# First unit in one written order, its second layer on whole float32 weights, and the weight splits moved behind it

## The chip, the cores and the metric

The kernel runs on one core of a Trainium2 chip. A time is the device time of one launch in microseconds (us); three launches before the change took 1181.29 to 1183.06 us, with a median of 1182.4. The traces come from one further launch under the profiler. Engines are named as the profile names them: PE (TensorE, matrix products), DVE (VectorE), ACT (ScalarE), POOL (GpSimd) and SP, whose queue issues every DMA.

## What is computed

```python
# x: (8 batches, 8 heads, 512 tokens, 64), state: (8, 8, 32, 64)
a  = softmax(x @ state.T / 8);   xread = a  @ state      # tokens read the state
a2 = softmax(state @ x.T / 8);   sread = a2 @ x          # the state reads the tokens
x  = concat(xread, sread) -> (8, 544, 512)
xn = (x - mean) / sqrt(var + 1e-6) * g_ln
x  = x + relu(xn @ w_ch1) @ w_ch2                        # 512 -> 2048 -> 512
h  = relu(x @ w_in);  c = conv3(h)                       # 512 -> 1024
out = (h * sigmoid(c)) @ w_out                           # 1024 -> 512
```

The weights arrive as float64, everything else as float32.

## The kernel before, in words

The work up to the second residual goes in nine units: one for the 512 tokens of each batch (units 0 to 7) and one for the 256 state rows of all batches together, which comes before unit 7. A unit has sixteen steps m. L1(u, m) (line 636) multiplies the attention weights `AH`/`AL` with the tile `ZH`/`ZL`, in which state and first weights are already multiplied together, into a PSUM bank `ph`; `relu_parts` (line 631) evicts it as a high part `hH` on ACT and a low part `hL` on DVE. L2(u, m) (line 652) multiplies both with slice m of the second weights into the four banks `acc`. `residual` (line 658) then scales `acc` on DVE, adds it to `XT` and stores it. On PE, a full-precision product of this kind is three matrix products of the type float32r: high times high, high times low, low times high (`three`, line 618). L1 takes six such products of 512 columns, L2 twelve. L1(u, m + 1) is issued ahead of L2(u, m), so that the eviction of one lies under the products of the other.

Unit 0 has work that the others lack, for the weights are made usable in it. A slice of 128 rows, 512 KB of float64, is turned into float32 in three stages: ACT takes the two words of each number apart (lines 199 and 200), DVE puts sign, exponent and mantissa in place (lines 205 and 206), POOL adds the last part (line 207). There are 32 slices, 16 of the first and 16 of the second weights. A slice of the second weights is then split into a high and a low float32r part, on ACT (line 239) and POOL (line 240). `z_first(j)`, four times in unit 0, takes four slices of the first weights: PE multiplies them with `gmean` (line 609, float32, 512 columns), DVE scales them and subtracts the product (line 612), PE multiplies them with the state (line 585), and ACT and DVE evict the result as `ZH` and `ZL` (lines 594 and 595). Their scaled form is stored to DRAM (`w1d`), and later units load it from there into a ring of seven buffers `r0` to `r6` (line 574). Beside this, unit 0 holds the layer norm of its own tokens and the attention of unit 1.

Each engine runs its instructions in one fixed order. In the first part of the launch (the attention of batch 0) and from unit 1 on, that is the order of the Python calls. `START` is such an order for the first part: each letter is one call of a generator. Unit 0 lies between the two and was ordered by a scheduler that goes by a model of the durations.

Of the kernel before, what the change touches and what calls it, by code (L numbers as in the profile page):

```python
# [9 lines left out]
F32 = mybir.dt.float32  # L10
# [32 lines left out]
def kernel(  # L43
# [28 lines left out]
    count = [0]  # L72
    hH = new("hH", [2, S], F32R)
    hL = new("hL", [2, S], F32R)
    XT = {}
# [12 lines left out]


    work = {**{c: f"b{c}" for c in "PQRUV"}, "s": "0"}  # L90

# [3 lines left out]
    RING, RAWS = 7, 5  # L95

    WARM = 8
    START = "s0w1ws0a1bab01ca01cabcabc"

# [501 lines left out]
    def z_first(j):  # L601


        for q in range(KC):
            need(1, KC * j + q)
        w = rounded[2 * j : 2 * j + 2]
        vp = bank()
        for q in range(KC):
            T.matmul(vp, gmean[:, q], w[q // 2][:, q % 2], start=q == 0, stop=q == KC - 1)
        for q in range(KC):  # L610
            t = w[q // 2][:, q % 2]
            V.scalar_tensor_tensor(t, t, gcol[:, q : q + 1], vp, op0=ALU.mult, op1=ALU.subtract)
        z_tiles(0, j, w)
        for g in range(2):
            nc.sync.dma_start(w1d[j, g], flat(w[g]))


# [10 lines left out]
    def hidden(m):  # L628
        return hH[:, m % 2], hL[:, m % 2]

    def relu_parts(m, p):
        h, l = (t[:, : p.shape[1]] for t in hidden(m))
        A.activation(h, p, AF.Relu)  # L633
        V.scalar_tensor_tensor(l, p, 0.0, f32(h), op0=ALU.max, op1=ALU.subtract)  # L634

    def L1(u, m):
        c = slice(P * (m % 4), P * (m % 4) + P)
        if u < NB:
            p = ph[m % 2]
            (wh, wl), (ah, al) = Z[u, m // 4], parts[u]  # L640
            for g in range(2):
                three(p, wh[:, g, c], wl[:, g, c], ah[:, g], al[:, g], g == 0, g == 1)
        else:
# [6 lines left out]
        relu_parts(m, p)  # L650
# [25 lines left out]
    w2 = {}  # L676

# [11 lines left out]

    AHEAD = 4  # L690

    def need(a, m):
        i = place_of[a, m]
        conv_a.ensure(min(i + AHEAD, conv_a.total - 1))
        return conv_a.done[i]

    def temp(i):
# [22 lines left out]
    tc_start.enter_context(tc.manual_schedule())  # L720
    V.memset(f32(hL), 0.0)
    G.memset(s_raw, 0.0)
# [43 lines left out]
    def warm(n):  # L766
        for _ in range(n):
            T.matmul(acc[3], hL[:, 1, :P], hL[:, 0], start=True, stop=True)

    warm(WARM)  # L770
    steps = {
        "s": state_start(),
        "0": tokens_start(0, x0T[0], sets[0]),
        "1": tokens_start(1, x0T[1], sets[1]),
    }
# [8 lines left out]
    tc_start.close()  # L784
    load_state(1)
    banks["free"] = pat

    round_1(craw, c0)
    round_2(craw, c0)

    def states_start():
        starts = [work, {"V": spare[5], "R": spare[6], "s": "1"}]
        E2Ts, z2s = [], []
        for g in range(2):
            sc = bank()
            for ql in range(2):
                q = 2 * g + ql
                for h in range(2):
# [3 lines left out]
                    )  # L802
            E2 = new(starts[g]["R"], [S])
            z2s.append(state_weights(sc, E2, starts[g]))
            E2Ts.append(state_weights_t(E2, starts[g]))
        yield
        srs = [state_read(0, g, E2Ts[g]) for g in range(2)]
        srzs = [state_scale(g, srs[g], z2s[g], starts[g]) for g in range(2)]
        yield
        for g in range(2):  # L810
            state_store(0, g, srzs[g])
        yield
        cp = bank()
        T.transpose(cp[:, :24], c0[:, 0], ident[:24, :24])
        A.activation(cw, cp[:, :24], AF.Copy)


# [52 lines left out]

    units = [*range(NB - 1), NB, NB - 1]
    LAST = units[-1]
    for u, follow in zip(units, [*units[1:], None]):
# [10 lines left out]
        made = []  # L884
        if u == 0:
            made += [(2, z_first, 1), (6, z_first, 2), (10, z_first, 3), (13, z_step, 1, 0)]
        elif u < NB:
            made += [(0, z_step, u, 1), (3, z_step, u, 2), (7, z_step, u, 3)]
            if u != LAST:
                made.append((10, z_step, LAST if follow == NB else follow, 0))  # L890

        def gap(m):
            if made and m >= made[0][0] and banks["held"] is None:
                _, make, *which = made.pop(0)
                make(*which)
            elif u == 0:
                with tc.high_priority(offset=100):
                    next(tasks, None)
            else:
                next(tasks, None)  # L900

        if u == 1:
            tc_start.enter_context(tc.manual_schedule())
        if u == 0:
            for g in range(2):
                token_read(0, g)
            for _ in states_start():
                pass
            z_first(0)
            L1(0, 0)  # L910
        for m in range(M1):
            if m < M1 - 1:
                L1(u, m + 1)
            if u == 0 and m == 3:
                for k in range(LATE, M1):
                    load_weight(place_of[2, k])
            if u == 0 and m == M1 - 4:
                pass_pairs(RING)
            if u == LAST:
# [10 lines left out]
            gap(m)  # L930
            if u == 0:
# [13 lines left out]
            if follow == NB and m % 3:  # L945
                gap(m)
        residual(u, n)
        if u != LAST:
# [3 lines left out]
    def place(m, shape, dt=F32):  # L952
        return new(f"w2_{m}", shape, dt)

# [140 lines left out]
```

## Time and profile before

| what | value |
|---|---|
| median of three launches | 1182.4 us |
| the profiled launch: its own time, its span | 1177.8 us, 1176.0 us |
| PE busy | 1125.9 us (96% of the span) |
| DVE busy | 726.6 us (62%) |
| ACT busy | 444.2 us (38%) |
| POOL busy | 207.8 us (18%) |
| mean granted clock of PE | 0.981 of full speed |

The span runs from the first to the last instruction of the trace; the launch's own time is 1.8 us longer. Shares over the whole span hide the stages: the start differs from the rest, and a table by stretches of the span shows it.

### The profile page before, as it was taken

To read this page: it belongs to the slowest core of one execution; us is meant where nothing else is said; L and a number is where in the kernel's file an instruction comes from. 1 tells how busy PE (TensorE), PEld (TensorE's weight loads), DVE (VectorE), ACT (ScalarE), POOL (GpSimd) and SP (SyncE) were. 2 spreads that over 40 slices of the span, in tenths; PEclk is the share of its full clock that TensorE was granted. 3 is DMA by queue.
4 is the path that set the end of the run, shared out by engine and by line. 5 is a ranking of instruction groups with operands and counts; after the bars stand their busy time and mean duration, and the time that the engine had idled before them with its cause. 6 is when DMAs were issued, how large, how long until landed. Compare 5 with 4: busy or idle time off the path is not lost.

```text
span 1176.0 us, 14628 instructions
## 1 busy us (share of the span) xinstructions
PE 1125.9 (96%) x5459; PEld 863.8 (73%) x5459; DVE 726.6 (62%) x1134; ACT 444.2 (38%) x788; POOL 207.8 (18%) x314
## 2 busy tenths in 40 slices
PE   5698899999999999999989999999999999999997
PEld 4365567777777777777767888788788888888885
DVE  4899666566566475565665622577677666666553
ACT  5665333323233233233233222565344434334332
POOL 2565400000000000000000000265433312213110
PEclk8699999999999999999999999999999999999999
DMA  9643533432243333334314124322112102100001
GB/s 298 206 171 108 158 96 105 108 95 90 72 109 85 81 111 76 78 120 108 95 56 107 38 101 155 119 72 90 37 54 72 37 37 80 37 36 36 1 37 45
DMA packets 129283, 106.31 MB, mean 90 GB/s; under 512 B 103332, under 2 KB 107452, under 8 KB 128188
## 3 DMA queue, kind: packets, MB, share of 16 engines
q1 hardware_dynamic: 129212, 105.37, 29.6%
q8 instruction: 43, 0.70, 0.2%
q14 instruction: 28, 0.23, 0.1%
HBM read 83.85 MB, written 21.50 MB: 90 GB/s over the span
## 4 chain that ended last, share of the span: by engine, by line
PE 80%; DVE 12%; ACT 3%; issue 2%; POOL 2%; SPq 0%; DMA 0%; ACTq 0%; DVEq 0%; POOLq 0%
PE acc L619 14%; PE acc L620 14%; PE acc L621 14%; PE ph L619 7%; PE ph L620 7%; PE ph L621 7%; PE pat L585 2%; PE pat L621 2%; PE pat L619 2%; PE pat L620 2%; PE pat L361 2%; PE ph L647 2%; DVE tn L500 1%; ACT bQ L488 1%; DVE ctmp L206 1%
## 5 line engine op out<-in xcount | busy, mean ns | idle before, releaser
L619 PE MATMUL acc<-hH,w 128*128 128x512 f32 (+1 forms) x576 | 221.6, 395 | 2.2 <-ACT hH L633 2.2
L620 PE MATMUL acc<-hL,w 128*128 128x512 f32 (+1 forms) x576 | 220.4, 383 | 1.8 <-DVE hL L634 1.7
L621 PE MATMUL acc<-hH,w 128*128 128x512 f32 (+1 forms) x576 | 220.1, 382 | 0.0
L634 DVE SCALAR_TENSOR_TENSOR hL<-ph,hH 128x512 fp32r<-128x512 f32 (+1 forms) x144 | 94.2, 657 | 183.4 <-ACT hH L633 183.2
L633 ACT ACTIVATE hH<-ph 128x512 fp32r<-128x512 f32 (+1 forms) x144 | 81.6, 569 | 208.9 <-PE ph L621 171.3
L619 PEld LDWEIGHTS acc<-hH,w 128*128 128x128 f32 x576 | 108.1, 188 | 54.5 <-issue 15.9
L1008 DVE SCALAR_TENSOR_TENSOR w<-w,cw,w 128x544 f32<-128x544 f32 x128 | 109.9, 860 | 38.0 <-POOL w L1006 36.2
L620 PEld LDWEIGHTS acc<-hL,w 128*128 128x128 f32 x576 | 109.2, 190 | 24.3 <-DVE hL L634 4.2
L621 PEld LDWEIGHTS acc<-hH,w 128*128 128x128 f32 x576 | 109.0, 189 | 21.7
L207 POOL TENSOR_TENSOR ctmp<-ctmp,AH 128x512 int32<-128x512 int32 x1 | 1.3, 1304 | 610.7 <-DVE ctmp L206 610.7
L619 PE MATMUL ph<-AH,ZH 128*128 128x512 f32 x256 | 104.3, 408 | 0.7 <-ACT ZH L594 0.7
L620 PE MATMUL ph<-AL,ZH 128*128 128x512 f32 x256 | 100.9, 394 | 0.0
L621 PE MATMUL ph<-AH,ZL 128*128 128x512 f32 x256 | 100.1, 395 | 0.0
L989 ACT ACTIVATE w<-w 128x544 f32<-128x544 f32 x64 | 42.1, 657 | 129.4 <-DVE w L1008 129.4
L996 DVE TENSOR_TENSOR w<-w,w 128x512 fp32r<-128x512 f32 x64 | 49.5, 774 | 42.9 <-ACT w L995 42.1
L990 DVE TENSOR_TENSOR w<-w,w 128x544 f32<-128x544 f32 x64 | 48.8, 762 | 39.5 <-ACT w L989 39.5
L619 PEld LDWEIGHTS ph<-AH,ZH 128*128 128x128 f32 x256 | 48.5, 190 | 19.5 <-issue 6.6
L995 ACT ACTIVATE w<-w 128x512 fp32r<-128x512 f32 x64 | 40.4, 631 | 52.4 <-DVE w L990 47.4
L1006 POOL TENSOR_SCALAR w<-w,cw 128x544 f32<-128x544 f32 x64 | 47.7, 746 | 61.8 <-ACT w L1002 58.4
L621 PEld LDWEIGHTS ph<-AH,ZL 128*128 128x128 f32 x256 | 48.2, 189 | 11.8 <-issue 0.8
L620 PEld LDWEIGHTS ph<-AL,ZH 128*128 128x128 f32 x256 | 48.6, 190 | 9.7
L997 POOL COPY w<-w 128x32 f32<-128x32 f32 x64 | 17.5, 273 | 177.5 <-DVE w L990 177.5
(439 smaller groups left out, 2182.0 us busy)
## 6 DMA issues: line engine op xcount, KB each, us to landing
r<-w1d SPq DMA_DIRECT2D x64, 512.0 KB, 4.5
out_dram<-w SPq DMA_DIRECT2D x34, 256.0 KB, 2.2
w<-in_moe_w_ch_dram SPq DMA_DIRECT2D x16, 512.0 KB, 8.0
r<-in_moe_w_ch_dram SPq DMA_DIRECT2D x16, 512.0 KB, 4.9
x2d<-XT SPq DMA_DIRECT2D x8, 1024.0 KB, 4.9
bP<-in_x_dram SPq DMA_DIRECT2D x112, 64.0 KB, 2.5
bP<-in_x_dram SPq DMA_DIRECT2D x28, 256.0 KB, 3.8
w1d<-r SPq DMA_DIRECT2D x8, 512.0 KB, 2.6
```

What stands on the lines that cost most here:

```text
L361: T.matmul(xr[ql], s[:, 2 * g + ql], a, start=i == 0, stop=i == 2)
L619: T.matmul(o, lh, rh, start=first, stop=False)
L620: T.matmul(o, lh, rl, start=False, stop=False)
L621: T.matmul(o, ll, rh, start=False, stop=last)
L633: A.activation(h, p, AF.Relu)
L634: V.scalar_tensor_tensor(l, p, 0.0, f32(h), op0=ALU.max, op1=ALU.subtract)
L989: A.activation(c, c, AF.Sigmoid)
L990: V.tensor_tensor(c, c, h[:, 1 : SEQ + 1], op=ALU.mult)
L995: A.activation(g[:, 0], c[:, :S], AF.Copy)
L996: V.tensor_tensor(g[:, 1], c[:, :S], f32(g[:, 0]), op=ALU.subtract)
L1006: G.tensor_scalar(c, h[:, 0:SEQ], cw[:, f : f + 1], 0.0, op0=ALU.mult, op1=ALU.add)
L1008: V.scalar_tensor_tensor(c, h[:, k : k + SEQ], cw[:, k * FF + f : k * FF + f + 1], c, op0=ALU.mult, op1=ALU.add,)
```

## The change

Unit 0 is no longer left to the scheduler. Its work is cut into generators, one per kind of work, and the string `START` calls them one after the other, a letter for each call: `a` and `b` are the stages of the conversion, `z` the two halves of `z_first`, `P` the products of unit 0, `T` the attention of unit 1, `N` the layer norm, `L` the token reads, `S` the state reads, `d` later loads, `c` splits.

In unit 0, L2 multiplies the whole float32 slice with a float32 `hH`: one product for each of the four banks instead of three, and no `hL`. Two slices share one buffer (`pair2`). The split of the second weights moves behind unit 0: slices 0 to 5 are split at its end (the letter `c`), slices 6 to 15 in unit 1, slice m + 2 after L2(1, m) from m = 4 on. The low part of a split is now subtracted on DVE instead of POOL.

```diff
...
-    hH = new("hH", [2, S], F32R)
-    hL = new("hL", [2, S], F32R)
+
+    hid = {c: new(f"h{c}", [2, S], F32 if c == "H" else F32R) for c in "HL"}
...
-    START = "s0w1ws0a1bab01ca01cabcabc"
+    START = "ss01abaa0b101aa0b1SabaSbzbaLLzPbSaPNSNbaSbPSbaSPdSPSadbPabNaaddbNzbPzPdNbNaabPNPPTPPaabTTTbaTPabPTbbadzzTbPTabTaabPPTaPaTdbPbbTTPTaTddPabzabPzPTPTaabbTPTPPcccPPbPPPTdPcccNTT"
+    SPLITS = 6
...
     def z_first(j):
 
 
-        for q in range(KC):
-            need(1, KC * j + q)
...
+        yield
...
+    def relu_parts(u, m, p):
+        if u == 0:
+            A.activation(hid["H"][:, m % 2], p, AF.Relu)
+            return
+        if (u, m) == (1, 0):
+            hid["H"] = new("hH", [2, S], F32R)
         h, l = (t[:, : p.shape[1]] for t in hidden(m))
         A.activation(h, p, AF.Relu)
         V.scalar_tensor_tensor(l, p, 0.0, f32(h), op0=ALU.max, op1=ALU.subtract)
...
     def L2(u, m, n):
         h, l = (t[:, :n] for t in hidden(m))
         for d in range(KC):
             c = slice(P * d, P * d + P)
-            three(acc[d][:, :n], w2[m][:, 0, c], w2[m][:, 1, c], h, l, m == 0, m == M1 - 1)
+            if u == 0:
+                T.matmul(acc[d], whole2[m][:, c], h, start=m == 0, stop=m == M1 - 1)
+            else:
+                three(acc[d][:, :n], w2[m][:, 0, c], w2[m][:, 1, c], h, l, m == 0, m == M1 - 1)
+
+    def split_w2(m):
+
+        w = w2[m] = new(slot2(m), [2, DM], F32R)
+        A.activation(w[:, 0], whole2[m], AF.Copy)
+        V.tensor_tensor(w[:, 1], whole2[m], f32(w[:, 0]), op=ALU.subtract)
...
+    w2, whole2, pair2 = {}, {}, {}
+
+    def slot2(m):
+        return f"w2_{(m + 7) % M1}" if m < M1 - 1 else "w2_e"
...
         if a == 2:
-            return None
+            if m % 2 == 0:
+                pair2[m // 2] = new(f"w2_{m // 2 - 1}" if m else "w2_e", [2, DM])
+            whole2[m] = pair2[m // 2][:, m % 2]
+            return whole2[m].rearrange("p (k c) -> p k c", c=P)
         if m % 2 == 0:
             rounded.append(new(f"r{RAWS + m // 2 % 2}", [2, S]))
-        if m + RAWS < M1:
-            load_weight(place_of[1, m + RAWS])
...
-    conv_steps = {"a": conv_a.first, "b": conv_a.second, "c": conv_a.third}
-    for c in START:
-        if c == "w":
-            warm(1)
-        elif c in steps:
-            next(steps[c], None)
-        else:
-            conv_steps[c]()
...
+    def firsts():
+        for _ in range(conv_a.total):
+            conv_a.first()
+            yield
+
+    def seconds():
+        for i, (a, m) in enumerate(order):
+            conv_a.second()
+            if a == 1 and m + RAWS < M1:
+                load_weight(place_of[1, m + RAWS])
+            yield
+
+    def firsts_made():
+        for j in range(KC):
+            yield from z_first(j)
+
+    def products_start():
+        L1(0, 0)
+        yield
+        for m in range(M1):
+            if m < M1 - 1:
+                L1(0, m + 1)
+                yield
+            L2(0, m, S)
+            yield
+        yield from residual(0, S)
+        z_step(1, 0)
...
+    def splits_start():
+        for m in range(SPLITS):
+            split_w2(m)
+            yield
...
+        "S": (states_start(), pat),
+        "z": (firsts_made(), pat),
...
+    for c in START:
+        banks["held"], banks["free"], banks["next"] = None, streams[c][1], turn.get(c, 0)
+        next(steps[c], None)
+        turn[c] = banks["next"]
...
+    splits = {(1, m): [m + 2] for m in range(SPLITS - 2, M1 - 2)}
...
-            if u == 0:
-                w2[m] = need(2, m)
             L2(u, m, n)
-            while u == 0 and made and made[0][0] < 12 and made[0][0] == m:
-                gap(m)
+            for k in splits.get((u, m), ()):
...
```

On PE, in the attention of batch 0 before: `L290`, `L300` and `L325` make the state's reads (`bV`, `w2_13`), `L609` multiplies the first weights (`r5`, `r6`) with `gmean`.

```order
L799 MATMUL pat0_83<-w2_10_34_175,sbd0_36_189 64x256
L799 MATMUL pat0_83<-w2_11_35_176,sbd0_36_189 64x256
L290 MATMUL pat1_84<-ident_8_70,w2_14_53_356 128x128 x4
L300 MATMUL pat0_83<-XT1_15_97,bV_52_350 64x128 x8
L300 MATMUL pat1_84<-XT1_15_97,w2_13_56_366 64x128 x8
L325 MATMUL pat0_83<-ident_8_70,bV_58_388 128x128
L325 MATMUL pat1_84<-ident_8_70,w2_13_60_394 128x128
L814 MATMUL pat0_83<-ident_8_70,cbuf_146 128x24
L609 MATMUL pat1_84<-r5_40_245,gmean_11_73 128x512 x2
L609 MATMUL pat1_84<-r6_45_284,gmean_11_73 128x512 x2
L585 MATMUL pat0_83<-r5_40_245,sbd0_36_189 32x512 x4
L585 MATMUL pat1_84<-r6_45_284,sbd0_36_189 32x512 x4
```

The same place in the changed kernel (its lines are numbered three to seven higher: `L612` is the former `L609`, `L366` the token read of line 361):

```order
L799 MATMUL pat1_84<-w2_10_34_175,sbd0_36_189 64x256
L799 MATMUL pat1_84<-w2_11_35_176,sbd0_36_189 64x256
L612 MATMUL pat0_83<-r5_38_217,gmean_11_73 128x512 x2
L612 MATMUL pat0_83<-r6_46_279,gmean_11_73 128x512 x2
L366 MATMUL acc0_77<-AH0_32_173,s_H_6_68 128x512
L366 MATMUL acc1_78<-AH0_32_173,s_H_6_68 128x512
L366 MATMUL acc0_77<-AH0_32_173,s_L_7_69 128x512
L366 MATMUL acc1_78<-AH0_32_173,s_L_7_69 128x512
L366 MATMUL acc0_77<-AL0_33_174,s_H_6_68 128x512
L366 MATMUL acc1_78<-AL0_33_174,s_H_6_68 128x512
```

The product with `gmean` now stands directly behind the scores of the state (`L799`) and ahead of the token reads; transposes and state reads, which stood ahead of it, come later.

On PE, step m = 4 of unit 0, the second layer before; `acc0` to `acc3` are the four banks, `w2_4_87` is the split slice:

```order
L619 MATMUL acc0_77<-hH_1_63,w2_4_87_577 128x512
L619 MATMUL acc1_78<-hH_1_63,w2_4_87_577 128x512
L619 MATMUL acc2_79<-hH_1_63,w2_4_87_577 128x512
L619 MATMUL acc3_80<-hH_1_63,w2_4_87_577 128x512
L620 MATMUL acc0_77<-hL_2_64,w2_4_87_577 128x512
L621 MATMUL acc0_77<-hH_1_63,w2_4_87_577 128x512
L620 MATMUL acc1_78<-hL_2_64,w2_4_87_577 128x512
L621 MATMUL acc1_78<-hH_1_63,w2_4_87_577 128x512
L620 MATMUL acc2_79<-hL_2_64,w2_4_87_577 128x512
L621 MATMUL acc2_79<-hH_1_63,w2_4_87_577 128x512
L620 MATMUL acc3_80<-hL_2_64,w2_4_87_577 128x512
L621 MATMUL acc3_80<-hH_1_63,w2_4_87_577 128x512
```

and changed, with the last three products of the first layer ahead of it; `w2_1_86` holds slices 4 and 5 whole:

```order
L624 MATMUL ph1_82<-AH0_32_173,ZH1_89_576 128x512
L625 MATMUL ph1_82<-AL0_33_174,ZH1_89_576 128x512
L626 MATMUL ph1_82<-AH0_32_173,ZL1_90_577 128x512
L667 MATMUL acc0_77<-hH_1_63,w2_1_86_543 128x512
L667 MATMUL acc1_78<-hH_1_63,w2_1_86_543 128x512
L667 MATMUL acc2_79<-hH_1_63,w2_1_86_543 128x512
L667 MATMUL acc3_80<-hH_1_63,w2_1_86_543 128x512
```

Twelve products have become four.

On DVE, the end of unit 0 before; `L670` scales the banks, `L672` adds, `L634` is `hL`, `L595` is `ZL`:

```order
L634 SCALAR_TENSOR_TENSOR hL_2_64<-ph0_81,hH_1_63 128x512
L670 TENSOR_TENSOR tn_174_1282<-acc0_77,rs0_72_485 128x512
L670 TENSOR_TENSOR tn_174_1282<-acc1_78,rs0_72_485 128x512
L672 TENSOR_TENSOR XT0_31_172<-XT0_31_172,tn_174_1282 128x512 x2
L670 TENSOR_TENSOR tn_174_1282<-acc2_79,rs0_72_485 128x512
L670 TENSOR_TENSOR tn_174_1282<-acc3_80,rs0_72_485 128x512
L672 TENSOR_TENSOR XT0_31_172<-XT0_31_172,tn_174_1282 128x512 x2
L634 SCALAR_TENSOR_TENSOR hL_2_64<-ph1_82,hH_1_63 128x512
L595 TENSOR_TENSOR ZL1_176_1319<-pat1_84,ZH1_175_1318 128x512
L595 TENSOR_TENSOR ZL1_176_1319<-pat0_83,ZH1_175_1318 128x512
```

and changed; `L675` is the new subtraction of a split, `L689` and `L692` the residual, `L600` and `L644` the former `L595` and `L634`:

```order
L675 TENSOR_TENSOR w2_7_155_1017<-w2_e_56_321,w2_7_155_1017 128x512
L675 TENSOR_TENSOR w2_8_156_1020<-w2_e_56_321,w2_8_156_1020 128x512
L675 TENSOR_TENSOR w2_9_157_1023<-w2_0_60_378,w2_9_157_1023 128x512
L210 TENSOR_SCALAR ctmp1_150_962<-ctmp1_150_962 128x512
L211 SCALAR_TENSOR_TENSOR ctmp1_150_962<-w2_15_142_887,ctmp1_150_962 128x512
L689 TENSOR_TENSOR tn_158_1048<-acc0_77,rs0_62_397 128x512
L689 TENSOR_TENSOR tn_158_1048<-acc1_78,rs0_62_397 128x512
L689 TENSOR_TENSOR tn_158_1048<-acc2_79,rs0_62_397 128x512
L689 TENSOR_TENSOR tn_158_1048<-acc3_80,rs0_62_397 128x512
L692 TENSOR_TENSOR XT0_31_172<-XT0_31_172,tn_158_1048 128x512 x4
L600 TENSOR_TENSOR ZL0_167_1105<-pat0_83,ZH0_166_1104 128x512
L600 TENSOR_TENSOR ZL0_167_1105<-pat1_84,ZH0_166_1104 128x512
L675 TENSOR_TENSOR w2_10_170_1114<-w2_0_60_378,w2_10_170_1114 128x512
L675 TENSOR_TENSOR w2_11_171_1117<-w2_1_86_543,w2_11_171_1117 128x512
L675 TENSOR_TENSOR w2_12_172_1120<-w2_1_86_543,w2_12_172_1120 128x512
L644 SCALAR_TENSOR_TENSOR hL_2_64<-ph0_81,hH_173_1129 128x512
```

Three splits stand ahead of the residual and three behind it, ahead of the first `hL` of unit 1.

## Rows read from the trace of the kernel before

**Rows 1.** Busy time by stretch: start:end, length, PE, PEld, DVE, ACT, POOL, PEclk, DMA, GB/s

```profile
20.00:40.00 20.00, 9.44 (x28) 5.71 (x28) 17.74 (x26) 14.51 (x29) 9.93 (x8) 0.59 0.80 236
40.00:60.00 20.00, 13.57 (x67) 7.66 (x67) 16.94 (x32) 12.49 (x24) 6.71 (x6) 0.69 0.73 246
60.00:80.00 20.00, 18.75 (x87) 11.63 (x86) 18.63 (x28) 14.19 (x24) 12.44 (x10) 1.00 0.60 210
80.00:100.00 20.00, 16.15 (x64) 12.02 (x63) 19.78 (x25) 10.93 (x20) 16.08 (x12) 0.91 0.46 131
...
120.00:140.00 20.00, 17.37 (x61) 12.43 (x62) 14.07 (x20) 7.30 (x13) 12.63 (x9) 0.91 0.56 130
```

**Rows 2.** Timeline of PE, 20 to 62: start, duration, instruction, idle before

```profile
24.07 1.11 PE L456 MATMUL pat<-ident,bU 128*128 128x128 f32 x4 [7.47 <-DVE bU L450]
...
47.35 1.11 PE L290 MATMUL pat<-ident,w 128*128 128x128 f32 x4 [4.27 <-ACT w L284]
...
53.96 3.70 PE L609 MATMUL pat<-r,gmean 128*128 128x512 f32 x8
...
61.47 0.50 PE L619 MATMUL ph<-AH,ZH 128*128 128x512 f32 x1
```

**Rows 3.** Timeline of POOL, 30 to 38

```profile
31.94 1.62 POOL L207 TENSOR_TENSOR r<-ctmp,r 128x512 int32<-128x512 int32 x1 [1.02 <-ACT XT L363]
...
35.63 1.40 POOL L207 TENSOR_TENSOR XTt<-XTt,w 128x512 int32<-128x512 int32 x1 [0.63 <-DVE XTt L206]
```

**Rows 4.** Timeline of DVE, 35 to 139

```profile
35.92 1.66 DVE L206 SCALAR_TENSOR_TENSOR ctmp<-w,ctmp 128x512 int32<-128x512 int32 x1
...
54.27 0.69 DVE L206 SCALAR_TENSOR_TENSOR ctmp<-r,ctmp 128x512 int32<-128x512 int32 x1
...
138.26 2.72 DVE L612 SCALAR_TENSOR_TENSOR r<-r,gcol,pat 128x512 f32<-128x512 f32 x4 [3.01 <-PE pat L609]
```

**Rows 5.** Timeline of PE, 92 to 173

```profile
92.19 1.08 PE L273 MATMUL pat<-bQ,sbd 128*64 128x512 f32 x4 [3.85 <-DVE bQ L369]
...
95.33 0.63 PE L621 MATMUL acc<-hH,w 128*128 128x512 f32 x1
...
134.63 3.59 PE L609 MATMUL pat<-r,gmean 128*128 128x512 f32 x8
...
141.04 0.39 PE L621 MATMUL acc<-hH,w 128*128 128x512 f32 x1
141.27 0.39 PE L619 MATMUL acc<-hH,w 128*128 128x512 f32 x1
...
172.91 0.50 PE L619 MATMUL acc<-hH,w 128*128 128x512 f32 x1
```

**Rows 6.** Groups of DVE instructions, 0 to 175: busy, mean ns, idle before

```profile
L205 DVE TENSOR_SCALAR ctmp<-ctmp 128x512 int32<-128x512 int32 x22 | 14.8, 675 | 1.5 <-ACT ctmp L199 1.5
L634 DVE SCALAR_TENSOR_TENSOR hL<-ph,hH 128x512 fp32r<-128x512 f32 x18 | 12.2, 682 | 8.5 <-ACT hH L633 8.5
L206 DVE SCALAR_TENSOR_TENSOR ctmp<-r,ctmp 128x512 int32<-128x512 int32 x11 | 12.2, 1107 | 0.2
```

**Rows 7.** Groups of POOL instructions, 0 to 175

```profile
L240 POOL TENSOR_TENSOR w<-ctmp,w 128x512 fp32r<-128x512 f32 x11 | 15.2, 1392 | 1.5 <-ACT w L239 1.5
...
L240 POOL TENSOR_TENSOR w<-XTt,w 128x512 fp32r<-128x512 f32 x5 | 7.1, 1425 | 0.3 <-ACT w L239 0.3
```

**Rows 8.** Timeline of ACT, 144 to 146

```profile
144.56 1.09 ACT L594 ACTIVATE ZH<-pat 128x512 fp32r<-128x512 f32 x2 [5.00 <-PE pat L585]
```

**Rows 9.** Timeline of SP's DMA issues, 35 to 164

```profile
35.59 4.62 SPq L141 DMA_DIRECT2D s_raw<-in_state_dram  x8
...
159.27 4.05 SPq L158 DMA_DIRECT2D bP<-in_x_dram  x8
```

**Rows 10.** DMA issues of the page: count, KB each, us to landing

```profile
r<-w1d SPq DMA_DIRECT2D x64, 512.0 KB, 4.5
```

**Rows 11.** Line 670: shortest, median and longest ns, first and last start

```profile
L670 DVE TENSOR_TENSOR tn<-acc,rs x28: 680/692/692, 168.6 to 664.3; 128x512 f32<-128x512 f32 x28
```

More of the change, by code (lines that the diff above doesn't have):

```diff
@@ L802, in states_start @@
                     )
[L803 to L809, printed above, removed]
+            E2s.append(new(starts[g]["R"], [S]))
+            z2s.append(state_weights(sc, E2s[g], starts[g]))
+            yield
+        for g in range(2):
+            E2T = state_weights_t(E2s[g], starts[g])
+            yield
+            sr = state_read(0, g, E2T)
+            srzs.append(state_scale(g, sr, z2s[g], starts[g]))
+            yield
         for g in range(2):
             state_store(0, g, srzs[g])
-        yield
+            yield
+        round_1(craw, c0)
+        round_2(craw, c0)
         cp = bank()
@@ L815, in states_start, with reads_start, loads_start, warm_steps @@
         A.activation(cw, cp[:, :24], AF.Copy)
+    def reads_start():
+        for g in range(2):
+            token_read(0, g)
+            yield
+    def firsts():
+        for _ in range(conv_a.total):
+            conv_a.first()
+            yield
+    def seconds():
[3 more added lines that the diff above has]
+                load_weight(place_of[1, m + RAWS])
+            yield
+    def firsts_made():
[3 more added lines that the diff above has]
+        L1(0, 0)
+        yield
+        for m in range(M1):
+            if m < M1 - 1:
+                L1(0, m + 1)
+                yield
+            L2(0, m, S)
+            yield
+        yield from residual(0, S)
+        z_step(1, 0)
+    def loads_start():
+        load_state(1)
+        yield
+        for m in range(LATE, M1):
+            load_weight(place_of[2, m])
+            yield
+        pass_pairs(RING)
+    def splits_start():
+        for m in range(SPLITS):
+            split_w2(m)
+            yield
+    def warm_steps():
+        while True:
+            warm(1)
+            yield
+    streams = {
+        "s": (state_start(), acc),
+        "0": (tokens_start(0, x0T[0], sets[0]), acc),
+        "1": (tokens_start(1, x0T[1], sets[1]), acc),
+        "a": (firsts(), acc),
+        "b": (seconds(), acc),
+        "L": (reads_start(), acc),
+        "S": (states_start(), pat),
+        "z": (firsts_made(), pat),
+        "P": (products_start(), pat),
+        "T": (attend(1), pat),
+        "N": (token_norm(0), pat),
+        "d": (loads_start(), acc),
+        "c": (splits_start(), acc),
+        "w": (warm_steps(), acc),
+    }
+    turn = {}
+    steps = {c: s[0] for c, s in streams.items()}
+    for c in START:
+        banks["held"], banks["free"], banks["next"] = None, streams[c][1], turn.get(c, 0)
+        next(steps[c], None)
+        turn[c] = banks["next"]
+    banks["free"], banks["held"] = pat, None
     x2, x2raw = {}, {}
@@ L884 @@
         made = []
-        if u == 0:
-            made += [(2, z_first, 1), (6, z_first, 2), (10, z_first, 3), (13, z_step, 1, 0)]
-        elif u < NB:
-            made += [(0, z_step, u, 1), (3, z_step, u, 2), (7, z_step, u, 3)]
+        if u < NB:
+            made += [(0, u, 1), (3, u, 2), (7, u, 3)]
             if u != LAST:
-                made.append((10, z_step, LAST if follow == NB else follow, 0))
+                made.append((10, LAST if follow == NB else follow, 0))
         def gap(m):
             if made and m >= made[0][0] and banks["held"] is None:
[L894 to L898, printed above, removed]
+                z_step(*made.pop(0)[1:])
             else:
                 next(tasks, None)
[L902 to L910, printed above, removed]
         for m in range(M1):
@@ L946 @@
                 gap(m)
-        residual(u, n)
+        for _ in residual(u, n):
+            pass
         if u != LAST:
@@ L952, in place @@
     def place(m, shape, dt=F32):
-        return new(f"w2_{m}", shape, dt)
+        return new(slot2(m), shape, dt)
     hb = [place(m, [HB]) for m in range(3)]
```

39 lines of the change are left out of this document (9 added, 30 removed).

## The prediction

> **What bounds the kernel now.** I read the table of busy time by stretches first [rows 1]. PE is busy 9.4 and 13.6 of 20 us up to 60 us, at a granted clock of 0.59 and 0.69, and 16 to 19 in the later stretches shown. DVE is busy 17 to 20 us of each stretch between 20 and 100. So the start is the one stage in which PE, which sets the pace of everything later, waits; whole units behind it are alike, since the six gaps between the residuals of units 0 to 6 add up to 664.3 - 168.6 = 495.7 us, 82.6 each [rows 11]. What a shorter start saves is saved at the end, if nothing in unit 1 eats it.
>
> Then the timeline of PE up to 62 us [rows 2]. It waits 7.5 us for the token softmax, and later 4.3 us in the state's softmax, one of several such waits there. The product with `gmean` starts at 53.96 and the first product of unit 0 at 61.47. Yet the four slices that this `gmean` needs are complete when POOL ends its fourth piece, at 31.94 + 1.62 = 33.56 [rows 3]. They lie ready for 20 us, because the fixed order of PE has the state's reads ahead.
>
> The stretch that I count goes from the first product of unit 0 (61.47) to the first L2 of unit 1 (172.91): 111.4 us [rows 2, 5]. Each 512-column product of the float32r kind takes 0.229 us from start to start (141.04 to 141.27). A float32 product of the `gmean` kind appears as two instructions: eight take 3.59 us, and less the last one's tail that is 0.857 us for a product (their eight starts are 0.43 apart; four products, 3.43 us) [rows 5]. The order has in this stretch 316 products of the first kind (72.4 us), 12 of the second (10.3), 40 small ones of line 585 (5.2), and transposes, scores and state reads (5.3): 93.2 us of work. The other 18.2 us are waits and low clock. An example is the wait of 3.85 us for DVE at 88.3; after it PE's products are 0.43 apart instead of 0.23, that is 1.2 instead of 2.4 GHz, and they last 0.63 us [rows 5].
>
> **The change part by part.** *L2 of unit 0* loses 16 x 12 float32r products, 192 x 0.229 = 44.0 us, and gains 16 x 4 float32 products, 64 x 0.857 = 54.8: 10.8 us more for PE. It is on the path, since PE leads there.
>
> *The new order* takes some work from before the first product of unit 0 to behind it: 16 state-read products, 8 transposes and a few small ones, some 3.4 us by the durations of the same rows. Work from the first product of unit 0 to the first L2 of unit 1 becomes 93.2 + 10.8 + 3.4 = 107.4 us.
>
> *The first product of unit 0* now follows the `gmean` of the first four slices, which stands right behind the scores. The fourth piece is rounded at about 30 us: before it is 33.56, and the softmax's idle on DVE is now filled by two conversions. Then come the last quarter of `gmean` (0.86, or 1.7 at the low clock), the twelve token reads (2.7 or 5.2), which hide DVE's four scalings of 2.72 us [rows 4], line 585 (1.1 or 2.1) and an eviction (0.55 us each, two in 1.09) [rows 8] with about 0.1 of delay. That gives 35.3 us at full clock and a piece at 30; 43.3 at low clock and a piece at 33.56. I take 41, near the late end, since the clock before was 0.59 and 0.69 there [rows 1].
>
> *The DVE* loses 16 evictions `hL` of 682 ns, 10.9 us [rows 6], and gains the splits, 16 subtractions, for which the nearest row is the same 0.68: three ahead of the residual (2.0 us), three behind it, ten in unit 1. *POOL* loses 16 subtractions, 15.2 + 7.1 us [rows 7]. That matters for DVE: line 206 takes 0.69 us while POOL rests, and 1.66 when it starts at 35.92 while POOL's addition runs from 35.63 to 37.03 [rows 3, 4]. So a conversion costs DVE its lines 205 and 206, 0.68 and 1.11 us in the largest groups [rows 6], some 1.73 on the mean of all, and 1.1 if POOL never stands in the way. I keep 1.73, although fewer POOL instructions remain.
> The Trainium skill, "SBUF — State Buffer", section "SBUF: two separate sides", says that DVE and GpSimd share a port pair that one of them holds for a whole instruction while the other is blocked. The trace agrees: the 1.66 ends when POOL's ends, plus 0.55. By that rule the missing 16 POOL instructions free DVE of more than I count, which is the first rival.
>
> *PE's waits in the new order.* (a) Second `gmean`: PE reaches it 16.2 us after the start (four L1, two L2, small ones), at 57.2. DVE has 20 us to do between the first `ZL` (42.5) and the last slice that it needs: six conversions (10.4) and 9.6 of norm, state and `ZL`; with POOL's 1.5 that is 64.0, and the last quarter ends at 64.9 where 60.6 would do: 4 us. (b) Then L2(0, 2) covers part of the scaling, but DVE has five other instructions ahead of it: 2.7. (c) Third `z_first`: nothing stands between `gmean` and line 585 on PE, so 2.72 of scaling, line 585 and the first evictions lie open, less some transposes: 2.9. (d) Third and fourth `gmean` wait 0.5 and 1.3 for POOL; the fourth `z_first` is covered by a product of 3.43 but for its eviction, 0.9. (e) Unit 0 ends with the token read, whose banks ACT has to clear (1.1 [rows 8]), then the state product of unit 1, `ZH`, and `ZL` behind the residual's eight DVE instructions of 0.69 (the first can begin while PE still works on the other banks): 1.9. The splits there run on ACT and DVE beside it. Sum 14.2. (f) Two of the waits throw PE to the low clock, as the one of 3.85 us did; that one ended at 92.19 and the product at 95.33 is still slow [rows 5], so about 3.7 us at half speed, which lose 1.85 each: 3.7. All in all 17.9 us, against 18.2 before.
>
> *Unit 1* gets ten splits, 0.69 on DVE and 0.55 on ACT each. They stand after a step's L2, when ACT and DVE wait for the next L1. Covered, they cost 0; each one whole in the way of an `hL` would cost 6.9. I take 0.6.
>
> Sum: 41 + 107.4 + 17.9 = 166.3 for the first L2 of unit 1, against 172.9: 6.6 us earlier, less 0.6: 6.0. The profiled launch goes from 1177.8 to 1171.8; the launches without the profiler stand 4.6 us above it, so the median goes from 1182.4 to 1176.4.
>
> **The rivals.** *First: DVE gets freer than I count.* Without POOL's 16 subtractions a conversion costs 1.3, between 1.1 and 1.73. The wait (a) loses 2.6, (b) and (d) about 3, and with shorter waits both falls of the clock (3.7): the loss is 8.6 instead of 17.9. With 40 for the start, PE arrives at 156: 16.9 earlier, 1182.4 - 16.3 = 1166. For it speaks the pair of rows with 0.69 and 1.66; against it, that DVE's scalings behind `gmean` remain.
>
> *Second, slower: the low clock.* Every one of the seven waits above throws PE back to 1.2 GHz, and then L2's products cost 1.71 instead of 0.857. Seven falls of 1.85 and 14.2 of waits are 27.2 us. The change loses from 172.9 - 41 - 107.4 = 24.5 us on; so it is 2.7 late, and with 0.6 in unit 1 the median is 1185.7. For it speaks the clock of 0.59 to 0.69 in the start [rows 1]; against it, that between 60 and 80 us it was 1.00 although PE was idle for 1.2 us of them.
> The Trainium skill, "TensorE: Matmul & The Clock Gate", section "HAM oscillation — how this bites in real kernels", tells of kernels in which every repeated wait returns PE to the low clock. The 3.85 us wait agrees with it; by that rule this rival is what happens.
>
> *Third, no change: SP's queue.* The state product of unit 1 needs `r0` and `r1` reloaded. SP issues this behind eight transfers of `bP`, which wait for a state read after L2(0, 11), and sixteen of the state: 4.05 + 2 x 4.62, then 4.5 to land: 17.8 us [rows 9, 10]. PE has three L1 and four L2 until then and a token read, 4.1 + 13.7 + 1.4 = 19.2. The margin is 1.4; if transfers that queue with them take 7.4 longer, margin and gain are gone, and the end is 1182.4.
>
> **How the numbers follow.** The forecast, 1171 to 1180, gets 0.50; the first rival 0.20; the third 0.15; the second 0.15. Differences of 0.2% (2.4 us) are about what can be told from no change here: faster 0.70, same 0.15, slower 0.15. The range goes from 1165, the first rival, to 1185, short of the whole of the second.
>
> **What would show it.** Right: the first `ph` product near 41 us (61.47 before); 128 instructions of the L2 line in unit 0, 0.43 apart; the first residual near 158 (168.6 before); the first L2 of unit 1 near 166; then units of 82.6. Wrong: a first product of unit 0 after 46; PE idle over 4 us in one piece; a granted clock under 0.9 between 60 and 160 (second rival); PE waiting for `r` from `w1d` at the unit's end (third); `hL` in unit 1 late behind a split.

## The result, and the profile after

The changed kernel takes 1164.8 us (median of four launches, 1163.2 to 1165.4); the kernel before 1181.9 (four launches). The ratio is 0.986, with a 95% interval of 0.9833 to 0.9886: 17 us faster, where 6 were forecast. The direction came as forecast; the size did not, and the median stands 0.2 us under the low end of the range. The price that comes nearest is that of the first rival, 1166.

The trace of the changed kernel has a span of 1163.6 us against 1176.0, 12.4 less. First its table by stretches, which answers to [rows 1] (columns as there).

```profile
20.00:40.00 20.00, 16.63 (x76) 9.73 (x76) 16.98 (x32) 13.47 (x26) 6.01 (x5) 0.81 0.92 276
40.00:60.00 20.00, 18.68 (x83) 10.04 (x82) 18.17 (x31) 11.71 (x23) 9.04 (x8) 1.00 0.35 114
60.00:80.00 20.00, 19.73 (x66) 9.21 (x64) 18.53 (x28) 11.53 (x20) 5.71 (x5) 1.00 0.70 232
80.00:100.00 20.00, 18.07 (x75) 7.98 (x74) 15.88 (x25) 8.94 (x16) 6.50 (x5) 1.00 0.52 170
...
120.00:140.00 20.00, 18.83 (x83) 9.44 (x82) 12.68 (x23) 6.68 (x13) 3.95 (x3) 1.00 0.32 82
```

PE is busy 16.6 and 18.7 us where it was 9.4 and 13.6, and from 40 to 160 us its granted clock is 1.00 in every stretch. DVE is as full as before up to 80 us, and less full later.

Then PE's timeline (start, duration, instruction, idle before and what ended it), which answers to [rows 2, 5].

```profile
28.41 3.67 PE L612 MATMUL pat<-r,gmean 128*128 128x512 f32 x8 [0.42 <-ACT bR L289]
...
36.60 0.50 PE L624 MATMUL ph<-AH,ZH 128*128 128x512 f32 x1 [0.64 <-ACT ZH L599]
...
49.39 0.33 PE L330 MATMUL pat<-ident,w 128*128 128x128 f32 x1 [1.32 <-DVE w L320]
...
55.22 3.59 PE L612 MATMUL pat<-r,gmean 128*128 128x512 f32 x8
...
89.78 1.13 PE L612 MATMUL pat<-r,gmean 128*128 128x512 f32 x2 [0.73 <-POOL r L212]
91.75 1.71 PE L590 MATMUL pat<-r,sbd 64*32 64x512 f32 x8 [0.84 <-DVE r L615]
...
103.60 0.33 PE L330 MATMUL pat<-ident,bV 128*128 128x128 f32 x1 [0.61 <-DVE bV L320]
...
124.73 0.50 PE L624 MATMUL ph<-AH,ZH 128*128 128x512 f32 x1 [0.69 <-ACT ZH L599]
...
152.33 1.55 PE L590 MATMUL pat<-r,sbd 64*32 64x512 f32 x16 [0.46 <-ACT XT L368]
...
158.37 0.50 PE L624 MATMUL acc<-hH,w 128*128 128x512 f32 x1
```

The first product of unit 0 starts at 36.60 instead of 61.47, the first L2 of unit 1 (the last row) at 158.37 instead of 172.91: 14.5 us earlier. Between the two PE has ten waits, 5.9 us in all; the longest of them is 1.32. Before, between the same two products, it had six, 8.7 us in all. Next the residuals (shortest, median and longest ns, first and last start; line 670 is now 689), and two groups of the conversion on DVE (line 205 is now 210, 206 is 211):

```profile
L689 DVE TENSOR_TENSOR tn<-acc,rs x28: 690/691/692, 147.9 to 651.7; 128x512 f32<-128x512 f32 x28
```

```profile
L210 DVE TENSOR_SCALAR ctmp<-ctmp 128x512 int32<-128x512 int32 x22 | 11.0, 502 | 0.9 <-ACT ctmp L204 0.9
...
L211 DVE SCALAR_TENSOR_TENSOR ctmp<-r,ctmp 128x512 int32<-128x512 int32 x11 | 8.9, 807 | 0.4
```

The first residual starts at 147.9, where I had it near 158, and the last at 651.7, 12.6 us before the 664.3 of [rows 11]. So 14.5 us are won at unit 1's first L2; unit 1 from there to its residual takes 76.9 us against 75.7 and gives 1.2 back, and the units behind it another 0.8. The mean of line 210 is 502 ns where it was 675, of line 211 807 where it was 1107 [rows 6]: over all groups of the two lines a conversion costs DVE 1.39 us instead of 1.73.

### The profile page after: what moved, and what is told of

Same layout as the page of the kernel before. It is cut to its first block, busy times and chain, and to the rows that moved or that the text cites. A ratio compares the mean times of both kernels' runs of the same rounds, so it can differ in the third digit from the quotient of the medians.

```text
span 1163.6 us, 14521 instructions
## 1 busy us (share of the span) xinstructions
PE 1128.9 (97%) x5393; PEld 845.3 (73%) x5393; DVE 720.9 (62%) x1134; ACT 442.2 (38%) x788; POOL 182.3 (16%) x298
## 5 line engine op out<-in xcount | busy, mean ns | idle before, releaser
L644 DVE SCALAR_TENSOR_TENSOR hL<-ph,hH 128x512 fp32r<-128x512 f32 (+1 forms) x128 | 83.4, 655 | 172.9 <-ACT hH L643 172.5
L624 PE MATMUL acc<-hH,w 128*128 128x512 f32 (+1 forms) x480 | 189.0, 394 | 0.0
L625 PE MATMUL acc<-hL,w 128*128 128x512 f32 (+1 forms) x480 | 181.8, 379 | 0.0
L626 PE MATMUL acc<-hH,w 128*128 128x512 f32 (+1 forms) x480 | 181.8, 379 | 0.0
L643 ACT ACTIVATE hH<-ph 128x512 fp32r<-128x512 f32 (+1 forms) x128 | 72.7, 568 | 196.3 <-PE ph L626 158.9
L624 PEld LDWEIGHTS acc<-hH,w 128*128 128x128 f32 x480 | 90.3, 188 | 44.7 <-issue 15.6
L626 PEld LDWEIGHTS acc<-hH,w 128*128 128x128 f32 x480 | 90.2, 188 | 18.2
L625 PEld LDWEIGHTS acc<-hL,w 128*128 128x128 f32 x480 | 90.3, 188 | 16.7 <-DVE hL L644 0.3
L667 PE MATMUL acc<-hH,w 128*128 128x512 f32 x112 | 50.4, 594 | 0.0
```

The source lines that it names most:

```text
L624: T.matmul(o, lh, rh, start=first, stop=False)
L625: T.matmul(o, lh, rl, start=False, stop=False)
L626: T.matmul(o, ll, rh, start=False, stop=last)
L667: T.matmul(acc[d], whole2[m][:, c], h, start=m == 0, stop=m == M1 - 1)
```

## The experiments

Each was timed in five rounds beside the kernel before on the same chip; medians of the kernel before were 1179.8 to 1181.5 there. The changed kernel's own 1164.8 comes from its first launches; timed once more at the end it took 1166.2, so a difference from it is good to some 1.5 us. The questions: which part brings the 17 us, and by what path.

**Order and arithmetic apart.** The first of two kernels keeps the new order and goes back to the old arithmetic.

```diff
-            if u == 0:
-                T.matmul(acc[d], whole2[m][:, c], h, start=m == 0, stop=m == M1 - 1)
-            else:
+            if True:
                 three(acc[d][:, :n], w2[m][:, 0, c], w2[m][:, 1, c], h, l, m == 0, m == M1 - 1)
...
             conv_a.second()
+            while conv_a.n2 < (i if i < 2 * M1 - 1 else 2 * M1):
+                third()
...
```

The step `third` splits a slice as before, the high part on ACT, the low part on POOL.

> The new order with the old arithmetic in unit 0: L2 as three float32r products a slice, hL made by DVE, each second weight split on ACT and POOL as it is converted. PE has 10.8 us less to do than in the changed kernel, DVE 10.9 us more (16 of 0.68), POOL 22.3 us more. Theory (the whole weights pay by what they take from DVE and POOL, which PE would wait for): PE's idle in unit 0 grows from 5.9 us to 16 or more, a granted clock of 0.5 comes back in places, and the time is 1166 to 1174. Rival (the order is all of the gain, the float32 products only cost): idle stays near 6 us and the time falls by about 10 us, to 1153 to 1157.

Measured: 1206.5 us, ratio 1.022 (1.0201 to 1.0241). Both expectations were too low; the rival is out. The groups of its waits from 30 to 195 us (who waited for what, us in total, times, longest):

```profile
POOL ctmp L212 <- DVE ctmp L211: 36.8, 7, 12.0
DVE hL L639 <- ACT hH L638: 28.5, 12, 4.9
ACT ctmp L204 <- POOL w L245: 20.5, 8, 5.5
ACT hH L638 <- PE ph L626: 17.4, 8, 6.8
...
POOL w L245 <- ACT w L244: 11.5, 4, 5.5
```

The old arithmetic makes a ring of waits: DVE stands for `hH`, which ACT makes from PE's `ph`; ACT stands for a temporary that POOL's subtraction holds; POOL stands for ACT's high part and, longest of all, for DVE's conversions. The places of the splits in this order were my own, so the 42 us over the changed kernel are the price of this order with them, not of every order.

The second keeps the old order (with its scheduler in unit 0) and takes the new arithmetic.

```diff
         if a == 2:
-            return None
+            if m % 2 == 0:
+                pair2[m // 2] = new(f"w2_{m // 2 - 1}" if m else "w2_e", [2, DM])
+            whole2[m] = pair2[m // 2][:, m % 2]
+            return whole2[m].rearrange("p (k c) -> p k c", c=P)
...
+    splits = {(0, 13): (0, 1, 2), **{(1, m): [m + 2] for m in range(4, M1 - 2)}}
```

> The old order with the new arithmetic: L2 of unit 0 with whole float32 weights, no hL, six slices split around unit 0's end, ten in unit 1. The first product of unit 0 stays near 61.5. Theory (the order brings the gain, the arithmetic alone does not): 10.8 us more for PE, of which at most the 8.8 us idle of the kernel before can be won back: 1182 to 1190, not under 1180. Rival (the arithmetic is the gain, since it frees DVE and POOL): 1165 to 1174.

Measured: 1186.0 us, ratio 1.0046 (1.0029 to 1.0063). The arithmetic alone costs 5.5 us, as the theory had it: 10.8 more for PE, half of it won back. The trace agrees: from the first product of unit 0 to the first L2 of unit 1 it takes 116.6 us, 5.2 more than before, with 4.7 us of waits on PE instead of 8.7 and a granted clock of 1.00 in every stretch from 80 us on, where two of [rows 1] have 0.91. So neither half, as built here, is a gain by itself, and together they win 17: the whole weights take away the waits that the early order ran into with the old arithmetic.

**What the removed DVE and POOL work was worth.** Three kernels put it back into the changed one, one kind at a time, with outputs that nothing reads. First the evictions `hL` of unit 0:

```diff
             A.activation(hid["H"][:, m % 2], p, AF.Relu)
+            V.scalar_tensor_tensor(hid["L"][:, m % 2], p, 0.0, hid["H"][:, m % 2], op0=ALU.max, op1=ALU.subtract)
             return
```

> The changed kernel plus the 16 hL evictions of unit 0 on DVE, which nothing reads: 10.9 us more for DVE, nothing for POOL or PE. If PE waits for DVE's sum of work, its idle between the first product and the first L2 of unit 1 grows by 4 us or more, up to 10.9: 1169 to 1176. If DVE has slack: 1164 to 1167.

Measured: 1181.8 us, 17 over the changed kernel; the whole gain is gone, more than the 10.9 us of work that came back. Its group of line 639, up to 180 us (busy, mean ns, idle before), and two of PE's waits:

```profile
L639 DVE SCALAR_TENSOR_TENSOR hL<-ph,hH 128x512 fp32r<-128x512 f32 x16 | 11.0, 685 | 18.5 <-ACT hH L638 18.5
```

```profile
97.13 1.12 PE L612 MATMUL pat<-r,gmean 128*128 128x512 f32 x2 [1.97 <-POOL r L212]
...
132.46 2.07 PE L612 MATMUL pat<-r,gmean 128*128 128x512 f32 x2 [4.20 <-POOL r L212]
```

DVE works 11.0 us on them and stands 18.5 us ahead of them. It runs its queue in order: the conversions behind an `hL` can't begin until PE has made `ph` and ACT `hH`, though they need neither. So DVE can't get ahead of PE, the last slices reach `gmean` late, and PE, which set the pace, waits in its turn. From the first product of unit 0 to the first L2 of unit 1 it takes 138.8 us by the trace, 17.0 more than in the changed kernel. None of PE's listed waits there is for an `hL` itself. The next kernel takes away that wait and leaves the work: the same number of instructions of the same kind and length, in the same places, on a tile at rest.

```diff
             A.activation(hid["H"][:, m % 2], p, AF.Relu)
+            l = f32(hid["L"][:, m % 2])
+            V.scalar_tensor_tensor(hid["L"][:, m % 2], l, 0.0, l, op0=ALU.max, op1=ALU.subtract)
             return
```

> The changed kernel plus 16 instructions on DVE in the places of the hL evictions of unit 0, of the same kind and length (some 0.69 us), but on a tile that is at rest: they wait neither for ACT nor for PE. Theory (what the evictions cost is DVE's wait for hH, in order, 18.5 us in the run that put them back, and not their 11 us of work): 1164 to 1169. Rival (the sum of DVE's work decides): as the run that put the evictions back, 1178 to 1182.

Measured: 1171.7 us (1170.7 to 1174.5).

```profile
L640 DVE SCALAR_TENSOR_TENSOR hL<-hL 128x512 fp32r<-128x512 f32 x16 | 10.9, 679 | 0.0
```

The busy time is the same, 10.9 us, the idle ahead of it 0.0. It lies between the two expectations: some 6.9 us of the 17.0 come with the work, some 10.1 with the wait. The traces give nearly the same shares: from the first product to the first L2 of unit 1 this kernel takes 128.3 us, 6.5 more than the changed one. The work's share holds a wait of PE of 1.96 us for POOL at the third `gmean`, and a granted clock of 0.50 from 94 to 98 us behind it. Then POOL's sixteen subtractions:

```diff
             conv_a.second()
+            if a == 2:
+                kc = lambda v: v.rearrange("p (k c) -> p k c", c=P)
+                G.tensor_tensor(kc(hid["L"][:, m % 2]), conv_a.tmp[i], kc(whole2[m]), op=ALU.subtract)
```

> The changed kernel plus 16 subtractions on POOL, one behind each converted second slice, whose output (in hL's place) nothing reads: some 22 us of POOL work as before, no more for DVE or PE. If DVE is freed by POOL's missing instructions (the first rival of the prediction, lines 210 and 211 stretched from 1.1 to 1.7 us while POOL runs), lines 210 and 211 get longer by 0.4 us and more a slice and PE's idle in unit 0 grows by 4 us or more: 1169 to 1176. If DVE has slack enough for it: 1164 to 1167.

Measured: 1170.5 us (1168.6 to 1171.3), 5.7 over the changed kernel. The time is where the first theory put it, but not by its path: line 211 goes from 807 to 884 ns, and a conversion costs 1.48 us instead of 1.39, not 0.4 more.

```profile
L211 DVE SCALAR_TENSOR_TENSOR ctmp<-r,ctmp 128x512 int32<-128x512 int32 x11 | 9.7, 884 | 0.4
```

So in the new order the missing subtractions explain 0.09 of the 0.34 us by which a conversion became shorter. That does not leave the rest to the order alone: the two kernels that changed one half each both have shorter conversions.

```profile
L206 DVE SCALAR_TENSOR_TENSOR ctmp<-r,ctmp 128x512 int32<-128x512 int32 x11 | 7.9, 725 | 0.1
```

```profile
L211 DVE SCALAR_TENSOR_TENSOR ctmp<-r,ctmp 128x512 int32<-128x512 int32 x11 | 7.6, 693 | 0.4
```

The first row is of the old order without the subtractions, the second of the new order with the old arithmetic and POOL's subtractions; over all groups a conversion takes 1.49 and 1.35 us there. Alone, then, the one takes off 0.24 us and the other 0.38, and both together 0.34: they do not add up. The second of these kernels waits much more, which by itself lets fewer instructions meet; which ones no longer do is not shown. The first L2 of unit 1 comes 6.0 us later (164.37), after 9.1 us of waits instead of 5.9 and one spell at the lower clock (0.57 from 95 to 99 us).

**The early first product.** The two steps of the first `z_first` and two L1 stand behind the state's reads again:

```diff
-... SabaSbzbaLLzPbSaPNSNbaSbPSbaSPdSPS ...
+... SabaSbbaLLbSaNSNbaSSzzPPbPbaSPdSPS ...
```

> The changed kernel with the first product of unit 0 put back: in the emitted order the two steps of the first z_first stand behind the state's reads, and the first two L1 behind them, as in the kernel before; all else as changed. First product near 50 to 54 instead of 36.6. If the early first product is worth what it is early (PE's own work sets the time from there on): 14 to 17 us slower, 1179 to 1182. Rival (DVE's conversions set the pace of unit 0, and they go on meanwhile): 1166 to 1172.

Measured: 1175.3 us (1172.1 to 1177.1), between the two. The first product starts at 50.57, 14.0 later, and the first L2 of unit 1 at 167.14, 8.8 later. Part of the 14 is only moved: state reads that now stand ahead of it stood behind it. The rest is waiting as of old, in front of them:

```profile
35.65 1.97 PE L305 MATMUL pat<-XT,bV 128*64 128x128 f32 x16 [4.95 <-ACT bV L297]
...
40.52 1.97 PE L305 MATMUL pat<-XT,w 128*64 128x128 f32 x16 [1.85 <-ACT w L297]
```

So the earlier first product is worth about two thirds of what it is earlier: 8.8 of 14.0 us by the trace.

**Can more be had?** Four kernels tried, and one joined two of them. Nine products that nothing reads, in PE's waits for the token softmax (`wwwwwww` and `ww` in `START`):

> The changed kernel plus nine products that nothing reads in PE's waits for the token softmax (18 to 23 us), where the granted clock is 0.5 until 27.6. If the low clock delays the first product of unit 0: the state's scores (3.5 us at 24.5) take half, the first product moves from 36.6 to about 35, and the time falls to 1163 or 1163.5. Rival (the fourth rounded piece and the softmax set that start): 1164.5 to 1166.

Measured: 1164.3 us (1163.5 to 1165.5). The granted clock of the stretch from 20 to 40 rises from 0.81 to 0.93, the first product comes at 35.97; 0.5 us is not to be told from nothing. Slices 13 to 15 back on three products:

```diff
-            if u == 0:
+            if u == 0 and m in THREE:
+                three(acc[d][:, :n], w2[m][:, 0, c], w2[m][:, 1, c], h, l, m == 0, m == M1 - 1)
+            elif u == 0:
...
```

> The changed kernel, with slices 13 to 15 split in unit 0 ahead of their L2, which is three float32r products again, with hL on DVE: 36 products of 0.229 us instead of 12 of 0.857, 2.0 us less for PE, and three splits fewer in unit 1. Where DVE idles (5.7 us at 134, 5.0 us at 143) an hL should cost nothing: 1162 to 1163.5. Rival (hL ties DVE and the residual behind it to PE here too): 1165 to 1168.

Measured: 1167.2 us (1165.8 to 1169.0), the time of the rival, but not its path. PE waits twice, and not for an `hL` but for the high part of a split, which it had not needed in unit 0 (line 683 is the split on ACT, 627 the first of the three products):

```profile
141.17 0.51 PE L627 MATMUL acc<-w,w 128*128 128x512 f32 x1 [1.20 <-ACT w L683]
150.52 0.51 PE L627 MATMUL acc<-w,w 128*128 128x512 f32 x1 [1.79 <-ACT w L683]
```

These 3.0 us are more than the 2.0 that the products save; the 1.0 that is left over lies within what can be told, so it is shown only that nothing is gained. The low part of the splits on POOL (`G` for `V` in `split_w2`):

> The changed kernel with the low part of all 16 splits subtracted on POOL instead of DVE (six at unit 0's end, ten in unit 1). Unit 1 from its first L2 to its residual took 76.9 us against 75.7 before. If the ten splits on DVE cost that 1.2: 1163 to 1164. If they are covered: 1164.5 to 1166. If POOL's longer subtraction holds DVE up at the unit's end: 1166 to 1168.

Measured: 1164.5 us (1163.8 to 1165.9), no change that can be told; unit 1 takes 76.3 us instead of 76.9. Three swaps of a scaling step with a conversion:

```diff
-... NSNbaSbPSbaSPd ... PTabTaabPP ... zPTPTaabbTPTPP ...
+... NSNbaSPSbbaSPd ... PTaTbaabPP ... zPTPTaabTbPTPP ...
```

> The changed kernel with three swaps in the emitted order: each time the step that scales a state read stands ahead of a conversion that it stood behind. PE waits for its output for 1.32, 0.61 and 0.48 us (at 49.4, 103.6 and 133.6), and line 318 takes 0.98 us on the mean beside POOL's addition, 0.23 without. If those waits go and nothing else becomes late: 2 us faster, 1162 to 1163.5. Rival (the conversions moved behind become late for the second gmean): 1165 to 1168.

Measured: 1164.3 us (1162.7 to 1165.2). The three waits are gone, but new ones of 1.22 and 0.35 us have come (at 51.3 and 116.7), and from the first product to the first L2 of unit 1 it is 120.8 us against 121.8. Last, these two together, beside the changed kernel itself:

> The changed kernel once more, unchanged, as the measure for the run beside it on the same chip: 1163 to 1166. If its launches, unlike those of the kernel before, have one granted clock, they lie within 3 us of each other.

> The three swaps of the scaling steps and the splits' low part on POOL together. Each alone came out 0.4 and 0.5 us under the changed kernel's median, which is not to be told from nothing. If the waits removed are worth their 1 us at unit 1's first L2 and add up with the splits: 1162 to 1163.5, and under the run beside it. Rival (no gain, launches scatter by as much): within 0.7 us of the run beside it.

Measured: 1166.2 us (1165.8 to 1167.1) for the changed kernel and 1164.5 (1162.7 to 1165.4) for the two edits. Beside each other the launches do not overlap. But the 1.8 us is below the 0.2% that I called the least difference to be told, it was measured once, and the changed kernel's first four launches (1163.2 to 1165.4) lie where those of the two edits lie. A gain is not shown.

## Why the prediction was right in direction and wrong in size

Forecast was 1176.4, measured 1164.8, 11.6 apart. They come from these steps:

- **The first product, 41 forecast, 36.6 measured: 4.4 us.** The steps of the sum were right: the fourth piece is rounded at 29.88 (28.59 + 1.29), "about 30".

```profile
28.59 1.29 POOL L212 TENSOR_TENSOR r<-ctmp,r 128x512 int32<-128x512 int32 x1 [2.03 <-DMA w<-in_moe_w_ch_dram]
```

  What failed is "near the late end, since the clock before was 0.59 and 0.69 there". From 28 us on the granted clock is 1.00, and the eight instructions with `gmean` take 3.67 us, full speed; the sum at full clock gave 35.3. With PE's waits for the state's reads back in front, in the kernel with the late first product, it is 0.74 from 30 to 50 us. So the low clock went with those waits, which the new order takes away; I carried a property of the old stretch into the new one.
- **From there to unit 1's first L2, 125.3 forecast, 121.8 measured: 3.5 us.** The work was 107.4 in the forecast and the loss 17.9. PE's listed waits are 5.9, and the line 590 behind a scaling is stretched (9.0 us busy for five times sixteen, where one undisturbed lot takes 1.09) by some 3.5 more; the remaining 5 us are spread over all kinds of products, and no run separates them. So the waits came out at 9.4 instead of 14.2, the two falls of the clock (3.7) did not come at all, and the work was undercounted by about 5, which hid a part of that. By the same rows (a) came to 0 instead of 4, (b) to 1.7 instead of 2.7, (c) to 2.8 instead of 2.9, (d) to 1.4 instead of 2.7, (e) to 1.2 instead of 1.9; another 2.4 are three waits for the scaling of a state read, which the list did not have.
- **Wait (a), the largest of the list**, is gone by three small margins. The row of PE at 55.22 has no idle. On DVE and POOL the stretch begins and ends with

```profile
36.58 1.29 DVE L600 TENSOR_TENSOR ZL<-pat,ZH 128x512 fp32r<-128x512 f32 x2 [0.54 <-ACT ZH L599]
```

```profile
56.01 1.29 POOL L212 TENSOR_TENSOR r<-XTt,r 128x512 int32<-128x512 int32 x1 [1.14 <-ACT hH L638]
```

  The first `ZL` starts with the first product, where I had it 1.5 us behind. DVE's six conversions take 8.4 us instead of 10.4, and with its other work and 1.2 us of its own waits it needs 19.3 us where I had 20. And PE comes to the second `gmean` 18.6 us after the first product, not 16.2. So the last slice, complete at 57.30, is there 0.5 us before PE takes it. The conversion was kept at 1.73 us, "although fewer POOL instructions remain"; it measured 1.39, and the first rival had 1.3.
- **"Loses 16 evictions `hL` of 682 ns, 10.9 us"** undervalues what the change takes away. Put back, they cost 17.0 us, of which some 6.9 go with the work and 10.1 with DVE's wait for `hH`. Such a wait stood in the rows that I quoted: behind the 682 of line 634 in [rows 6] is "8.5 <-ACT hH". I read the mean and left the idle out, as if a wait of an engine that isn't the bottleneck cost nothing. It did, for conversions stood behind it that PE needed. The waits (a) to (e) were summed for the new order, without any `hL`, so this is not what made them too large; it is the part of the mechanism that the prediction did not see.
- **L2 on whole float32 slices costs PE 10.8 us**: held. The 64 products take 0.86 each as forecast, and the arithmetic alone made the old order 5.5 us slower, where 4.0 us of PE's waits went in exchange.
- **Unit 1 loses 0.6**: it lost 1.2, and the units behind it 0.8 that I had not counted. With the splits on POOL unit 1 lost 0.6, so by these single traces about half of the 1.2 is DVE's part in them. The 4.4 and 3.5 us of the first two points less these 1.4 are the 6.4, rounded, by which the profiled launch came earlier than I had it: 1165.4 against 1171.8. One reading was off without entering the sum: 664.3 is the start of the last of unit 6's four scalings, which begin at 662.2, so the six gaps are 82.3 us each and not 82.6.
- **"The launches without the profiler stand 4.6 us above it"**: the remaining 5.2 us. In the changed kernel the profiled launch lies 0.6 above the median, not 4.6 below. The kernel before scatters with the clock that it is granted. Of its 48 launches beside the experiments, the 12 with a mean clock under 0.976 took 1182.7 us on the mean, the 14 from 0.976 to 0.978 took 1180.9, the 17 at 0.979 and 0.980 took 1179.5, and the 5 above took 1177.9. Its profiled launch, 1177.8 at 0.981, was one of the fastest. The nine launches of the changed kernel have 0.987 to 0.994 and lie within 4 us. So the two profiled launches differ by 12.4 us and the medians by 17; the 4 to 5 us between go with a lower granted clock in most launches of the kernel before. Where in those launches it falls, no trace shows.

Of the rivals, the second, a fall of the clock at every wait, did not come: its trace would have had a clock under 0.9 between 60 and 160 us, and it has 1.00 in every stretch shown there. In the kernel with `hL` back, the granted clock is 0.95, 0.88 and 0.91 in the three stretches from 80 to 140 us: the waits of 1.97 and 4.20 us were each followed by a spell at 1.2 GHz, one of 2.54 us at 151 was not, and in the changed kernel none of the ten shorter ones was. With POOL's subtractions back, the clock fell at 95 us with no wait over 1.1 us near it, so the length of one wait does not decide alone. The Trainium skill, "TensorE: Matmul & The Clock Gate", section "HAM oscillation — how this bites in real kernels", tells of a kernel in which each of many repeated waits for a DMA returns PE to the low clock; the prediction stretched that to all seven waits here, most of them short. In the trace with `hL` back it held for two of the three longest waits, in the changed kernel for none of the ten. The third, SP's queue, did not come either: the state product of unit 1 waits 0.46 us, for ACT, not for its reload.

The first rival gave 1166 by "DVE gets freer than I count". It has the right engine and nearly the right conversion; the runs add that the larger part of what the evictions cost is the order in which DVE waits. That its number comes so near is in part luck: it too adds the 4.6 us between profiled launch and median, which did not hold. Its first L2 of unit 1 was at 156, measured 158.37, and its profiled launch would be 1161.5, measured 1165.4. By the Trainium skill, "SBUF — State Buffer", section "SBUF: two separate sides", a DVE instruction with two inputs in SBUF is blocked while a GpSimd instruction that reads SBUF holds the port pair that they share; the runs agree in kind, but sixteen more POOL instructions made a conversion only 0.09 us longer.

## What to carry to other kernels

An instruction on an engine that runs its queue in order costs its duration and also the wait that it imposes on everything behind it, even on an engine that is not the bottleneck: read the idle beside a group as well as its mean, and ask who needs what stands behind. Two edits can each lose, as these two did in the forms tried, and together win: an early order needs engines that can run ahead, so price the pair and not only the parts. And before a single profiled launch is set against a median, look at how the launches scatter, and with what.

## What the runs showed that I had not expected

- One DVE instruction in a step, 0.68 us, cost 1.06 us of the launch when it waited for two other engines, and 0.43 when the same work waited for nothing (17.0 and 6.9 us for sixteen of them).
- The launch time of the kernel before follows its mean granted clock, 1182.7 us under 0.976 and 1177.9 above 0.980, though its instructions are the same each time.
- Sixteen POOL subtractions (22 us) cost 5.7 us of the launch while DVE's conversions became only 0.09 us longer each; in the old order, taking them away together with the `hL` made a conversion 0.24 us shorter.
